# One load for the Q weights, the safe program laid ahead of each engine's last part, and the last output tile opened earlier, in a one-core attention kernel

## The chip, the core and the metric

The kernel runs on one core of a Trainium2 chip. The core has TensorE (PE in the profile, with PEld for its weight loads), VectorE (DVE), ScalarE (ACT), GpSimd (POOL) and SyncE (SP). They share an on-chip memory, and PE writes its results to eight accumulator banks (PSUM) of 128 x 512 float32. SP and ScalarE issue the transfers to and from the chip's main memory, which 16 DMA engines carry out. The instructions of each engine come from main memory as well, and the profile lists the packets that fetch them as queues of the kind "instruction". The metric is the device time of one execution in microseconds, as the median of several runs.

## The reference

A multi-head attention block with one sequence of 2048 rows, 448 features and 16 heads of 28 features. Inputs are bfloat16: `x` [1, 2048, 448], `wqkv` [448, 1344], `wo` [448, 448].

```python
qkv = transpose((x @ wqkv).reshape(B, S, 3, H, Dh), (2, 0, 3, 1, 4))
q, k, v = qkv[0], qkv[1], qkv[2]
scores = einsum("bhqd,bhkd->bhqk", q, k) * (Dh ** -0.5)
p = softmax(scores, axis=-1)
o = einsum("bhqk,bhkd->bhqd", p, v)
out = transpose(o, (0, 2, 1, 3)).reshape(B, S, D) @ wo
```

## The kernel before

The launch holds two programs. `_fast` computes the softmax without subtracting a maximum; at its end it checks that all row sums lie in a safe interval and writes the answer to `FLAG`. `_general`, the safe program, computes the same with a maximum and is run only where the check fails. `body` (line 1608) lays both out for each engine: the engine's instructions of `_fast`, a wait for `FLAG`, a load of its value into a register (line 1611), a branch (line 1612) to the label `done_` of that engine or to its `safe_` block, then the safe program, then `done_`. With the given inputs the branch to `done_` is taken. The safe program is long, and it lies between the branch and its target. A branch can be given a hint: `emit_engine` marks a place in an engine's stream ahead of the operation named in `HINT_AT`, and the hint instruction stands there (line 292; for GpSimd at the end of its operations, line 315). Behind `done_`, SP waits for the output's transfers (line 1627), and all engines meet in a final barrier (L1594 in the profile, a drain and semaphores).

**The order of work** is made by a planner written in Python, `_Prog.schedule`, which runs when the kernel is built. Each operation has an engine, its dependencies, an estimated duration and a priority (a lower number goes first). On each engine the planner takes, among the operations that can start within 150 ns of the first, the one with the lowest priority number, and among equals the one that was added first. PE's accumulator banks come from pools. Where the plan leaves PE a gap, it fills in passes on zeros (`zero_pass`, line 463), which serve only to keep PE's clock up. The order so found is fixed: each engine runs its list in order, waiting on semaphores.

**Loads** (lines 423 to 437). `x` comes in pieces of 256 or 512 rows, `wqkv` in three parts t = 0 (Q), 1 (K), 2 (V), seen as four row blocks of 112. In the order of issue SP loads x rows 256 to 511, the second halves of K's and Q's weights, x 512 to 1023, x 1024 to 1535, V's weights, x 1536 to 2047, then 16 pieces of `wo`. ScalarE issues x rows 0 to 255 and the first halves of K's and Q's weights.

**Head.** PE transposes x (`tr_job`, line 527: one job is one row block of 112 features for 512 rows), VectorE or ScalarE copies the result out of PSUM to `xT`, PE multiplies it with the weights (`proj_qk`, line 544: four steps of four matmuls that run side by side; `proj_v`, line 561), and the results are copied to `QT`, `KT`, `V`. For the first 512 rows the transposed block 1 is copied by ScalarE, the other three by VectorE; K's and Q's first projections have the same priority, Q's is added first and copied by ScalarE, K's by VectorE. These jobs take their banks from a pool of three. Later projections are spread over the rest of the run.

**Main part.** The work has 16 units: four groups of four heads, times four chunks of 512 query rows. A unit has 64 score tiles of 128 keys x 512 queries (16 key tiles, 4 heads). PE makes the scores (line 854), and ScalarE exponentiates three tiles at a time (two in unit 0), line 877; the operations are named E0, E1, and so on. About one tile in eight goes to VectorE instead, which evaluates a polynomial (lines 899 to 919). PE then multiplies the exponentials with V and adds over the 16 key tiles in one bank: the passes PV{unit}_{key tile}, line 810. A column of ones in V gives the row sums.

**Behind each unit** (`post_unit`): VectorE copies the sums out, SP sends them through main memory (`L1_`, `L2_`, `L3_`, `L4_`), VectorE takes reciprocals and normalizes (`NM{unit}`, line 733). When the last head group of a query chunk is done, PE multiplies with `wo` (line 703), VectorE copies the output tile out (`OPEV{tile}`, line 691) and SP stores it (`ODMA{tile}`, line 693).

**Tail** (`last_unit`). The last unit, 15, ends with output tiles 12 to 15. PE opens each of them with the product over the first three head groups (`OPA{tile}_{group}`, line 752, priority -34.0), as banks are free. The row sums go through PE here (N1 and N2, lines 771 and 786), VectorE normalizes in two halves (`NM15_0`, `NM15_1`), PE adds the last group (`OPB12` to `OPB15`, line 795, priority -35), ScalarE copies and stores tiles 12 and 14, VectorE copies tiles 13 and 15 and SP stores them. The check is a matmul on PE (`CKS`, line 947, priority -34.5) and one instruction on VectorE that writes `FLAG` (line 950). PE's order at the end is OPA12, OPA13, PV15_15, OPA14, N1, N2, OPB12, OPB13, OPB14, CKS, OPA15, OPB15.

Of the kernel before, what the change touches and what calls it, by code (L numbers as in the profile page):

```python
# [62 lines left out]
class _Prog:  # L63
# [12 lines left out]
    WINDOW = 3413.0  # L76
    FILL = None
    HINT_AT = {}
    FILL_DUR = 235.0
    FILL_ACT = 512.0  # L80
    FILL_TARGET = 5600.0
# [202 lines left out]
                    c += 1  # L284
                    op.count = c

    def emit_engine(self, e, engine, sems):
        waited = {}
        hint = None
        for op in self.order[e]:  # L290
            if op.name == self.HINT_AT.get(e):
                hint = engine.mark_branch_hint_location()
            need = {}
            for d in op.deps:
                if d.dma_group is not None:
                    key = ("dma", id(d.dma_group))
                    val = 16 * d.dma_index
                    sem = d.dma_group.sem
                else:
                    key = ("eng", d.eng)  # L300
                    val = d.count
                    sem = sems[d.eng]
                if waited.get(key, 0) >= val:
                    continue
                if key not in need or need[key][1] < val:
                    need[key] = (sem, val)
            for key, (sem, val) in need.items():
                engine.wait_ge(sem, val)
                waited[key] = val
            ins = op.emit(engine)  # L310
            if op.dma_group is not None:
                ins.then_inc(op.dma_group.sem, 16)
            elif op.sig:
                ins.then_inc(sems[e], 1)
        return engine.mark_branch_hint_location() if hint is None and self.HINT_AT else hint


RLO = 2.0 ** -40
# [18 lines left out]
def _fast(nc, x, wqkv, wo, out, n_heads=16):  # L337
# [28 lines left out]
    NU = len(units)  # L366
# [3 lines left out]
    P = _Prog()  # L370
    es = ExitStack()
    with es:
# [53 lines left out]
        def load_w(en, t, i0, i1):  # L426
            return load(en, (lambda e: e.dma_start(w_raw[0:IT, i0:i1, t * D:(t + 1) * D], wview[:, i0:i1, t * D:(t + 1) * D])),  # L427
                        f"w{t}_{i0}", (i1 - i0) * IT * D * 2)
        dma_x.append([load_x("act", 0, 2), load_x("sp", 2, 4)])
        for t in (1, 0):  # L430
            dma_w[t] = [load_w("act", t, 0, 2), load_w("sp", t, 2, 4)]
        dma_x.append([load_x("sp", 4, 8)])
        dma_x.append([load_x("sp", 8, 12)])
        dma_w[2] = [load_w("sp", 2, 0, 4)]
# [134 lines left out]

        for c in range(NCH):  # L570
            for it in range(NIT):
                tr_job(4 * c, it, -3 + 0.001 * it if c == 0 else 0.25 * c - CFG["klead"] + 0.001 * it, "act" if (c == 0 and it == 1) else "dve")
            if c == 0:
                proj_qk(0, 0, 0, -2.9, True, "act")
                proj_qk(1, 0, 0, -2.9, True, "dve")
            else:
                proj_qk(1, 0, c, 0.25 * c - CFG["klead"] + 0.05, True)
            proj_v(0, c, 0.25 * c + CFG["vlag"], True)
# [162 lines left out]
        def last_unit(u, last_pv):  # L741
            g, c = units[u]
            ub = u % 2
            pr = u - 50.0
            open_ops = []
            for j in range(NQT):
                n = c * NQT + j
                hold = []

                for gg in range(G - 1):  # L750
                    def f_part(e, n=n, hold=hold, gg=gg):
                        return e.matmul(bank(hold[0].banks[0])[:, 0:D], OTN[:, gg, n * 128:(n + 1) * 128], wop[:, gg, :],  # L752
                                        start=(gg == 0), stop=False, skip_group_check=True)
                    op = P.add("pe", f_part, deps=([otn_ev[(g_, c)] for g_ in range(G - 1)] + dma_wo[-1:] + mid_ev) if gg == 0 else [], after=hold[-1:], kind="f", units=0.9, act=448.0,
                               prio=-34.0, name=f"OPA{n}_{gg}", acq=("T", 1) if gg == 0 else None)
                    if gg == 0:
                        hold.append(op)
                open_ops.append((n, hold, op))
            HF = QCH // 2
            evs = []  # L760
            for k in range(2):
                sl = slice(k * HF, (k + 1) * HF)
                evs.append(P.add("dve", (lambda e, sl=sl: e.tensor_copy(OTS[:, ub, sl], bank(pv_open[u].banks[0])[:, sl])),
                                 deps=[last_pv, ots_last[ub]], after=evs[-1:], dur=340, prio=pr, name=f"ACCEV{u}_{k}", rel=[(pv_open[u], 0)] if k else []))
            n1s, rss, n2s, nms = [], [], [], []
            for k in range(2):
                def f_n1(e, k=k):
                    b = n1s[k].banks[0]
                    ins = None
                    for qt in (2 * k, 2 * k + 1):  # L770
                        ins = e.matmul(bank(b)[:, qt * 4:(qt + 1) * 4], OTS[:, ub, qt * 128:(qt + 1) * 128], SEL[:, :], start=True, stop=True)  # L771
                    return ins
                n1s.append(P.add("pe", f_n1, deps=[evs[k], sel_op], after=n1s[-1:], dur=430, prio=pr, name=f"N1_{u}_{k}", acq=("T", 1)))
            for k in range(2):
                i0 = u * 16 + 8 * k
                rss.append(P.add("dve", (lambda e, k=k, i0=i0: e.reciprocal(RS[:, i0:i0 + 8], bank(n1s[k].banks[0])[:, 8 * k:8 * k + 8])),
                                 deps=[n1s[k]], after=rss[-1:], dur=120, prio=pr, name=f"RS{u}_{k}", rel=[(n1s[k], 0)]))
                rs_last.append(rss[-1])

                def f_n2(e, k=k):  # L780
                    b = n2s[k].banks[0]
                    ins = None
                    for qt in (2 * k, 2 * k + 1):
                        for h in range(4):
                            i = u * 16 + qt * 4 + h
                            ins = e.matmul(ps[32 * h:32 * h + 32, b * 512 + qt * 128:b * 512 + (qt + 1) * 128],  # L786
                                           RS[:, i:i + 1].to_broadcast([128, 32]), id_f[:, :], start=True, stop=True, tile_position=(0, 32 * h))
                    return ins
                n2s.append(P.add("pe", f_n2, deps=[rss[k]], after=n2s[-1:], dur=480, prio=pr, name=f"N2_{u}_{k}", acq=("M", 1)))
                sl = slice(k * HF, (k + 1) * HF)  # L790
                nms.append(P.add("dve", (lambda e, sl=sl, k=k: e.tensor_tensor(OTN[:, g, c * QCH + sl.start:c * QCH + sl.stop], bank(n2s[k].banks[0])[:, sl], OTS[:, ub, sl], ALU.mult)),  # L791
                                 deps=[n2s[k]], after=nms[-1:], dur=340, prio=pr, name=f"NM{u}_{k}", rel=[(n2s[k], 0)]))
            for j, (n, hold, op) in enumerate(open_ops):
                def f_fin(e, n=n, hold=hold):
                    return e.matmul(bank(hold[0].banks[0])[:, 0:D], OTN[:, g, n * 128:(n + 1) * 128], wop[:, g, :], start=False, stop=True, skip_group_check=True)  # L795
                fin = P.add("pe", f_fin, deps=[nms[j // 2]], after=[op], kind="f", units=0.9, act=448.0, prio=pr, name=f"OPB{n}")
                out_tile(n, fin, hold[0], "act" if j % 2 == 0 else "dve", pr)

        def pv(u, kt):
# [154 lines left out]
        P.FILL = zero_pass  # L954
        P.START, P.COLD, P.HOT_UNTIL = 750.0, 7500.0, 10500.0
        n0 = (NCH - 1) * NQT
        P.HINT_AT = {"pe": f"OPA{n0}_0", "dve": f"OPEV{n0 - 1}", "act": f"OPEV{n0}", "sp": f"ODMA{n0 + 1}"}
        P.schedule()

        P.assign()  # L960
# [629 lines left out]
def _mha(nc, x, wqkv, wo, out, n_heads=16):  # L1590
# [3 lines left out]
    with es:  # L1594
# [11 lines left out]
        block = es.enter_context(nc.Block())  # L1606

        def body(e, eng):
            hint = F.emit_engine(e, eng, fs)
            eng.wait_ge(fs["dve"], F.flag_op.count)  # L1610
            ok = eng.value_load(F.flag_ap)
            eng.br_ne(ok, 0, on_true=f"done_{e}", on_false=f"safe_{e}").branch_hint(hint)
            with nc.body(f"safe_{e}", valid_engines=[eng.engine]):
                if e == "sp":
                    for gr in F.finish:
                        eng.wait_ge(gr.sem, 16 * gr.n)
                eng.drain().then_inc(bar, 1)
                eng.wait_ge(bar, 5)
                R.emit_engine(e, eng, rs)
                if e == "sp":  # L1620
                    for gr in R.finish:
                        eng.wait_ge(gr.sem, 16 * gr.n)
                eng.br(f"done_{e}")
            nc.switch_bb(f"done_{e}")
            if e == "sp":
                for gr in F.finish:
                    eng.wait_ge(gr.sem, 16 * gr.n)
# [52 lines left out]
```

## Time and profile before

| what | value |
|---|---|
| median of 3 runs | 421.03 us (420.53 to 422.55) |
| the profiled execution's own time | 424.5 us |
| its span, first to last instruction | 422.7 us |
| granted clock of PE, mean over the span | 0.996 |
| busy: PE, VectorE, ScalarE, GpSimd | 380.2, 385.5, 402.9, 3.4 us |
| ScalarE's exponentials | 307, 399.4 us in all |
| instruction packets, queue q8 and queue q14 | 36 and 13 |

The profiled execution is one run; its span leaves out 1.8 us of its own time, and it is 3.5 us above the median of the other runs. In a row of the profile "L877 ACT ACTIVATE PT<-ps" means: line 877 of the kernel, on ScalarE, reads `ps` (PSUM) and writes `PT`. "[2.51 <-PE ps L854]" means that the engine had been idle for 2.51 us and that an instruction of line 854 on PE ended it. An engine with a small q, as in SPq, is the engine's sequencer, which issues transfers, waits and branches.

### The profile page before, as it was taken

Reading aid. Unit: us, or ns where it says so; the run is one execution under the profiler, and the core shown is the slowest. Engines: PE = TensorE matmul, PEld = TensorE weight load, DVE = VectorE, ACT = ScalarE, POOL = GpSimd, SP = SyncE. Lnnn points to the kernel's source line nnn. Section 1 sums busy time; section 2 is a strip of 40 time slices with the busy share of each in tenths; the row PEclk is TensorE's granted clock in tenths of the full one; section 3 lists DMA queues with packets and bytes.
Section 4 is the critical chain, followed back from the end, with each engine's and each line's share of the span. In section 5 each row is a group of like instructions: output and inputs, shape, how many; then the busy total and the mean of one; then the engine's idle time right before and its main releaser. Section 6 shows DMA issues by size and latency. Waiting matters only on the chain.

```text
span 422.7 us, 9986 instructions
## 1 busy us (share of the span) xinstructions
PE 380.2 (90%) x4419; PEld 122.4 (29%) x4419; DVE 385.5 (91%) x608; ACT 402.9 (95%) x312; POOL 3.4 (1%) x9
## 2 busy tenths in 40 slices
PE   6999898899999898998989899989989998898895
PEld 3433222322323223232322222223222322222232
DVE  4489999999999999999999999999999999999923
ACT  2799999999999999999999999999999999999991
POOL 3000000000000000000000000000000000000000
PEclk9899999999999999999999999999999999999999
DMA  8200000101010000100001010000000001100111
GB/s 262 65 2 2 5 26 3 27 0 29 2 26 5 4 26 2 29 2 18 13 3 27 2 28 2 4 26 4 27 2 27 2 6 25 36 28 24 59 44 51
DMA packets 13897, 10.28 MB, mean 24 GB/s; under 512 B 5980, under 2 KB 11868, under 8 KB 13848
## 3 DMA queue, kind: packets, MB, share of 16 engines
q1 hardware_dynamic: 12808, 8.72, 7.6%
q10 hardware_dynamic: 1040, 0.86, 0.6%
q8 instruction: 36, 0.59, 0.6%
q14 instruction: 13, 0.11, 0.1%
HBM read 7.50 MB, written 2.08 MB: 23 GB/s over the span
## 4 chain that ended last, share of the span: by engine, by line
ACT 93%; PE 3%; DMA 2%; DVE 0%; ACTq 0%; issue 0%
ACT PT L877 93%; DMA w_raw<-in_wqkv_dram 2%; PE ps L544 1%; PE ps L752 1%; PE ps L854 0%; PE ps L810 0%; PE ps L527 0%; PE ps L795 0%; PE ps L703 0%; PE ps L771 0%; PE ps L463 0%; DVE OUTS L691 0%; PE ps L786 0%; ACTq L427 0%; ACTq L424 0%; DVE OTN L791 0%
## 5 line engine op out<-in xcount | busy, mean ns | idle before, releaser
L877 ACT ACTIVATE PT<-ps 128x1536 bf16<-128x1536 f32 (+1 forms) x307 | 399.4, 1797 | 2.5 <-PE ps L854 2.5
L854 PE MATMUL ps<-QT,KT 28*128 28x512 bf16 x1024 | 152.5, 384 | 31.4 <-ACT PT L877 28.2
L463 PE MATMUL ps<-ZM,ZW 128*32 128x512 bf16 x1404 | 113.8, 388 | 1.4 <-DVE ZM L445 1.2
L810 PE MATMUL ps<-PT,V 128*32 128x512 bf16 x890 | 96.0, 388 | 2.3 <-DVE OTS L716 1.1
L899 DVE TENSOR_SCALAR DT<-ps 128x512 f32<-128x512 f32 x134 | 91.3, 684 | 2.7 <-PE ps L854 1.5
L854 PEld LDWEIGHTS ps<-QT,KT 28*128 28x128 bf16 x1024 | 37.4, 91 | 164.9 <-ACT PT L877 130.8
L919 DVE SCALAR_TENSOR_TENSOR PD<-DT,DU 128x1024 int16<-128x1024 f32 x67 | 81.7, 1219 | 1.2
L810 PE MATMUL ps<-PD,V 128*32 128x512 bf16 x134 | 50.9, 388 | 0.0
L917 DVE TENSOR_TENSOR DU<-DU,DW 128x1024 f16<-128x1024 f16 x67 | 46.2, 689 | 1.7
L913 DVE TENSOR_TENSOR DU<-DW 128x1024 f16<-128x1024 f16 x67 | 46.0, 686 | 1.5
L911 DVE TENSOR_SCALAR DW<-DT 128x1024 f16<-128x1024 uint16 x67 | 45.5, 680 | 0.2
L463 PEld LDWEIGHTS ps<-ZM,ZW 128*32 128x32 bf16 x1404 | 34.7, 96 | 37.3 <-issue 19.9
L810 PEld LDWEIGHTS ps<-PT,V 128*32 128x32 bf16 x890 | 23.9, 93 | 51.5 <-issue 39.0
L544 PE MATMUL ps<-xT,w_raw 112*32 112x512 bf16 x512 | 35.3, 390 | 2.0 <-DMA w_raw<-in_wqkv_dram 1.8
L915 DVE TENSOR_SCALAR DU<-DU 128x1024 f16<-128x1024 f16 x67 | 27.9, 416 | 0.8
L515 DVE CAST KT<-ps 128x512 bf16<-128x512 f32 x16 | 11.0, 685 | 7.6 <-PE ps L544 7.4
L561 PE MATMUL ps<-w_raw,xT 112*128 112x112 bf16 x256 | 16.4, 214 | 0.2 <-DVE DT L899 0.2
L544 PEld LDWEIGHTS ps<-xT,w_raw 112*32 112x32 bf16 x512 | 11.5, 97 | 16.4 <-issue 3.5
L691 DVE CAST OUTS<-ps 128x448 bf16<-128x448 f32 x14 | 8.7, 622 | 7.2 <-PE ps L703 6.6
L561 PEld LDWEIGHTS ps<-w_raw,xT 112*128 112x128 bf16 x256 | 12.9, 98 | 5.9 <-issue 4.2
L810 PEld LDWEIGHTS ps<-PD,V 128*32 128x32 bf16 x134 | 12.1, 93 | 7.8 <-issue 6.6
L703 PE MATMUL ps<-wop,OTN 128*128 128x448 bf16 x48 | 11.3, 355 | 0.0
(47 smaller groups left out, 96.0 us busy)
## 6 DMA issues: line engine op xcount, KB each, us to landing
RB<-scr_r SPq DMA_DIRECT2D x60, 64.0 KB, 2.0
out_dram<-OUTS SPq DMA_DIRECT2D x14, 112.0 KB, 1.7
x_nat<-in_x_dram SPq DMA_DIRECT2D x3, 448.0 KB, 8.9
w_raw<-in_wqkv_dram SPq DMA_DIRECT2D x2, 196.0 KB, 5.3
w_raw<-in_wqkv_dram ACTq DMA_DIRECT2D x2, 196.0 KB, 5.7
w_raw<-in_wqkv_dram SPq DMA_DIRECT2D x1, 392.0 KB, 9.6
wop<-in_wo_dram SPq DMA_DIRECT2D x16, 24.5 KB
scr_l<-OTS SPq DMA_DIRECT2D x15, 8.0 KB
```

Source lines behind the costliest of these rows:

```text
L463: ins = e.matmul(ps[32 * h:32 * h + 32, b * 512:(b + 1) * 512], ZW[:, :], ZM[:, :], start=shut, stop=shut, skip_group_check=not shut, tile ...
L544: ins = e.matmul(ps[32 * h:32 * h + 32, b * 512:(b + 1) * 512], w_raw[0:IT, it, col:col + 32], xT[0:IT, it, c * 512:(c + 1) * 512], start= ...
L561: ins = e.matmul(ps[:, b * 512 + j * GD:b * 512 + (j + 1) * GD], xT[0:IT, it, n * 128:(n + 1) * 128], w_raw[0:IT, it, 2 * D + g * GD:2 * D ...
L810: ins = e.matmul(ps[32 * h:32 * h + 32, b * 512:(b + 1) * 512], V[:, kt, hh * 32:(hh + 1) * 32], p_ap, start=(kt == 0), stop=(kt == NK - 1 ...
L854: ins = e.matmul(bank(b), KT[32 * h:32 * h + rows, g, kt * 128:(kt + 1) * 128], QT[32 * h:32 * h + rows, g, c * QCH:(c + 1) * QCH], start= ...
L877: ex = P.add("act", (lambda e, p0=p0, w=w, bf=bf: e.activation(PT[:, p0 * 512:(p0 + w) * 512], bank(bf(), w), AF.Exp, scale=ESCALE)), deps ...
L899: o1 = P.add("dve", (lambda e, T1=T1, s=s: e.tensor_scalar(T1, bank(s.banks[0]), ZLO, ZOFF, ALU.max, ALU.add)), deps=[s, d_last[di]], dur= ...
L911: o2 = P.add("dve", (lambda e, F16=F16, W=W: e.tensor_scalar(W, F16, ES, EC, ALU.mult, ALU.add)), deps=[o for _, o, _ in pair] + [d_last[d ...
L913: o3 = P.add("dve", (lambda e, W=W, U=U: e.tensor_tensor(U, W, W, ALU.mult)), deps=[o2], dur=65 + n * 0.521, prio=pr, name=f"D3_{gi}")
L915: o4 = P.add("dve", (lambda e, U=U: e.tensor_scalar(U, U, EP, None, ALU.add)), deps=[o3], dur=65 + n * 0.261, prio=pr, name=f"D4_{gi}")
L917: o5 = P.add("dve", (lambda e, W=W, U=U: e.tensor_tensor(U, U, W, ALU.mult)), deps=[o4], dur=65 + n * 0.521, prio=pr, name=f"D5_{gi}")
L919: o6 = P.add("dve", (lambda e, U=U, T=T, O=O: e.scalar_tensor_tensor(O, T, ZFIN, U, ALU.add, ALU.add)), deps=[o5] + [slot_last.get(("D", q ...
```

## The change

Three things are changed.

- **Loads.** The Q weights come in one load of all four row blocks, issued by SP behind its half of K's weights and ahead of x's rows from 512 on; ScalarE's load of them is gone. The copy of the transposed block 1 moves from ScalarE to VectorE. K's first projection goes ahead of Q's (priorities -2.9 and -2.8).
- **Layout.** Each engine's stream is cut ahead of one operation (`JUMP_AT`; for GpSimd behind its last). There an unconditional branch goes to a new label `tail_`, and the safe program stands between this branch and the tail. The rest of the fast program follows at `tail_`, and behind it the wait for `FLAG`, the load of its value, the branch, and directly behind the branch the label `done_`. The cut is ahead of PV8_11 on PE, OPEV11 on VectorE, E0 on ScalarE, and the first `L1_0` on SP. A hint for the new branch is given on PE (ahead of PV8_8) and on VectorE (ahead of NM14); the others have none, and the closing branch has none.
- **Tail.** OPA's priority becomes -34.9, and that of OPB14 and OPB15 becomes -34.8.

```diff
-        for t in (1, 0):
-            dma_w[t] = [load_w("act", t, 0, 2), load_w("sp", t, 2, 4)]
+        dma_w[1] = [load_w("act", 1, 0, 2), load_w("sp", 1, 2, 4)]
+        dma_w[0] = [load_w("sp", 0, 0, 4)]
...
-                tr_job(4 * c, it, -3 + 0.001 * it if c == 0 else 0.25 * c - CFG["klead"] + 0.001 * it, "act" if (c == 0 and it == 1) else "dve")
+                tr_job(4 * c, it, -3 + 0.001 * it if c == 0 else 0.25 * c - CFG["klead"] + 0.001 * it, "dve")
             if c == 0:
-                proj_qk(0, 0, 0, -2.9, True, "act")
                 proj_qk(1, 0, 0, -2.9, True, "dve")
+                proj_qk(0, 0, 0, -2.8, True, "act")
...
-                               prio=-34.0, name=f"OPA{n}_{gg}", acq=("T", 1) if gg == 0 else None)
+                               prio=-34.9, name=f"OPA{n}_{gg}", acq=("T", 1) if gg == 0 else None)
...
-                fin = P.add("pe", f_fin, deps=[nms[j // 2]], after=[op], kind="f", units=0.9, act=448.0, prio=pr, name=f"OPB{n}")
+                fin = P.add("pe", f_fin, deps=[nms[j // 2]], after=[op], kind="f", units=0.9, act=448.0, prio=pr if j < 2 else -34.8, name=f"OPB{n}")
...
-        P.HINT_AT = {"pe": f"OPA{n0}_0", "dve": f"OPEV{n0 - 1}", "act": f"OPEV{n0}", "sp": f"ODMA{n0 + 1}"}
+        P.HINT_AT = {"pe": "PV8_8", "dve": f"NM{NU - 2}"}
+        P.JUMP_AT = {"pe": "PV8_11", "dve": f"OPEV{n0 - 1}", "act": "E0", "sp": "L1_0"}
...
+            def jump(hint):
+                br = eng.br(f"tail_{e}")
+                if hint is not None:
+                    br.branch_hint(hint)
+                with nc.body(f"safe_{e}", parent=top, valid_engines=[eng.engine]):
...
+                nc.switch_bb(f"tail_{e}", parent=top)
+
+            F.emit_engine(e, eng, fs, jump)
             eng.wait_ge(fs["dve"], F.flag_op.count)
             ok = eng.value_load(F.flag_ap)
-            eng.br_ne(ok, 0, on_true=f"done_{e}", on_false=f"safe_{e}").branch_hint(hint)
...
-            nc.switch_bb(f"done_{e}")
+            eng.br_ne(ok, 0, on_true=f"done_{e}", on_false=f"safe_{e}")
+            nc.switch_bb(f"done_{e}", parent=top)
```

In `emit_engine` the call `jump(hint)` comes ahead of the operation named in `JUMP_AT`, or behind the engine's last one where none is named.

More of the change, by code (lines that the diff above doesn't have):

```diff
@@ L78 @@
     HINT_AT = {}
+    JUMP_AT = {}
     FILL_DUR = 235.0
@@ L285, in assign, with emit_engine @@
                     op.count = c
-    def emit_engine(self, e, engine, sems):
+    def emit_engine(self, e, engine, sems, jump=None):
         waited = {}
@@ L292, in emit_engine @@
                 hint = engine.mark_branch_hint_location()
+            if op.name == self.JUMP_AT.get(e):
+                jump(hint)
+                jump = None
             need = {}
@@ L314, in emit_engine @@
                 ins.then_inc(sems[e], 1)
-        return engine.mark_branch_hint_location() if hint is None and self.HINT_AT else hint
+        if jump is not None:
+            jump(hint)
 RLO = 2.0 ** -40
@@ L1608, in body @@
         def body(e, eng):
-            hint = F.emit_engine(e, eng, fs)
+            top = nc.cur_bb
+            def jump(hint):
[3 more added lines that the diff above has]
+                with nc.body(f"safe_{e}", parent=top, valid_engines=[eng.engine]):
+                    if e == "sp":
+                        for gr in F.finish:
+                            eng.wait_ge(gr.sem, 16 * gr.n)
+                    eng.drain().then_inc(bar, 1)
+                    eng.wait_ge(bar, 5)
+                    R.emit_engine(e, eng, rs)
+                    if e == "sp":
+                        for gr in R.finish:
+                            eng.wait_ge(gr.sem, 16 * gr.n)
+                    eng.br(f"done_{e}")
+                nc.switch_bb(f"tail_{e}", parent=top)
+            F.emit_engine(e, eng, fs, jump)
             eng.wait_ge(fs["dve"], F.flag_op.count)
             ok = eng.value_load(F.flag_ap)
[L1612 to L1623, printed above, removed]
-            nc.switch_bb(f"done_{e}")
+            eng.br_ne(ok, 0, on_true=f"done_{e}", on_false=f"safe_{e}")
+            nc.switch_bb(f"done_{e}", parent=top)
             if e == "sp":
```

## The prediction

> **What bounds the kernel now.** I read the page first (the chain that ended last, the costliest groups, the queues), then the first 16 us and the last 20 us in order of time, then the branches and the transfers around them.
>
> ```profile
> span 422.7 us, 9986 instructions
> ...
> q8 instruction: 36, 0.59, 0.6%
> ...
> ACT 93%; PE 3%; DMA 2%; DVE 0%; ACTq 0%; issue 0%
> ...
> L877 ACT ACTIVATE PT<-ps 128x1536 bf16<-128x1536 f32 (+1 forms) x307 | 399.4, 1797 | 2.5 <-PE ps L854 2.5
> ```
>
> ScalarE's exponentials are 93% of the chain, and 2.5 us before the first of them is all the idle time ahead of 307. Nothing in the change makes an exponential shorter or fewer. What can move is when the first one starts, what comes after the last, and whether a jump in the middle breaks the row. In order of time, the head (start, duration, engine, line):
>
> ```profile
> 2.24 1.03 SPq L424 DMA_DIRECT2D x_nat<-in_x_dram  x2
> 8.85 2.67 PE L544 MATMUL ps<-xT,w_raw 112*32 112x512 bf16 x28 [1.82 <-DMA w_raw<-in_wqkv_dram]
> 10.44 0.17 PEld L544 LDWEIGHTS ps<-xT,w_raw 112*32 112x32 bf16 x4 [0.26 <-issue]
> 11.45 1.10 PE L527 MATMUL ps<-id_b,x_nat 128*112 128x128 bf16 x8
> 12.96 0.39 PE L854 MATMUL ps<-QT,KT 28*128 28x512 bf16 x4
> 13.39 17.52 ACT L877 ACTIVATE PT<-ps 128x1024 bf16<-128x1024 f32 x19 [2.51 <-PE ps L854]
> ```
>
> The first exponential starts at 13.39. Behind it stand the Q weights (PE waits until 8.85), 28 projection matmuls, transposes of the next x rows (11.45), one pass on zeros and the first scores at 12.96. The tail, first in order of time, then the closing branch (L1612), the first instruction behind it (L1594), and SP's wait for the last store:
>
> ```profile
> 410.36 0.62 DVE L691 CAST OUTS<-ps 128x448 bf16<-128x448 f32 x1 [2.30 <-PE ps L703]
> 415.96 0.80 PE L795 MATMUL ps<-wop,OTN 128*128 128x448 bf16 x3
> 416.79 0.74 PE L752 MATMUL ps<-wop,OTN 128*128 128x448 bf16 x3
> 417.37 0.35 PE L795 MATMUL ps<-wop,OTN 128*128 128x448 bf16 x1
> 417.76 0.62 DVE L691 CAST OUTS<-ps 128x448 bf16<-128x448 f32 x1 [0.53 <-PE ps L795]
> L1612 PEldq COMPARE_BRANCH  x1: 396/396/396, 417.8 to 417.8; - x1
> L1612 DVEq COMPARE_BRANCH  x1: 84/84/84, 418.5 to 418.5; - x1
> L1612 ACTq COMPARE_BRANCH  x1: 68/68/68, 419.2 to 419.2; - x1
> L1594 PEldq DRAIN  x1: 62/62/62, 418.3 to 418.3; - x1
> L1594 ACTq DRAIN  x1: 81/81/81, 420.2 to 420.2; - x1
> L1594 DVEq DRAIN  x1: 58/58/58, 422.2 to 422.2; - x1
> SPq L1627 <- DMA out_dram<-OUTS: 2.4, 1, 2.4
> ```
>
> All arithmetic is over at 417.76 + 0.62 = 418.4, and the span ends at 422.7: 4.3 us go to the closing branch and the last stores. Two things end together at 422.2. VectorE branches at 418.5 and runs the instruction behind the branch only at 422.2, 3.7 us later; ScalarE needs 1.0 (419.2 to 420.2), PE 0.5. And SP waits 2.4 us for the last output. How long the output stores take to land, and the instruction packets of the same stretch. The store issued at 408 us:
>
> ```profile
> out_dram<-OUTS SPq DMA_DIRECT2D x1, 112.0 KB, 1.7
> ```
>
> That of 411 us, with one instruction packet in the stretch to 412.9:
>
> ```profile
> q8 instruction: 1, 0.02, 4.1%
> ...
> out_dram<-OUTS SPq DMA_DIRECT2D x1, 112.0 KB, 3.5
> ```
>
> That of 417.2, ahead of the branches, and then the last, issued at 418.4, with the packets from 418.35 to the end:
>
> ```profile
> out_dram<-OUTS SPq DMA_DIRECT2D x1, 112.0 KB, 2.0
> ```
>
> ```profile
> q14 instruction: 6, 0.05, 3.1%
> q8 instruction: 1, 0.02, 2.2%
> ...
> out_dram<-OUTS SPq DMA_DIRECT2D x1, 112.0 KB, 3.8
> ```
>
> With no instruction packet beside it a store lands after 1.7 us; with a single one it took 3.5, and the last, among seven, 3.8. So the closing branches seem to cost twice: the fetch itself, and the late share of the last store that runs beside the fetches.
>
> **The change, part by part.** *The tail.* With the safe program moved ahead, the final branch goes to the instruction behind it, so neither the 3.7 us of VectorE nor the fetches should be there. PE's order also changes: OPA15 (priority -34.9) comes ahead of OPB14 and OPB15 (-34.8) and of the check CKS (-34.5). OPB12 and OPB13 stay at 415.96 and 0.2 later; OPA15's three matmuls take 416.79 to 417.37 = 0.58 now and would run from 416.36; OPB14 follows at 416.94, OPB15 at 417.14, 0.23 before 417.37. Tile 14's product is later than now, but done near 417.3, before VectorE's last copy. That copy and SP's last store, now at 417.76 + 0.62 + 0.03 = 418.41, move by 0.23: the store starts at 418.18. FLAG now falls behind that copy, near 418.3; every engine's closing branch waits for it, but SP reads it only after issuing its store, and the other engines have until the store lands. I let it land after 2.0, the row of the same stage: 420.2 instead of 422.2. Term: **-2.0 us**; bounds with 1.7 (419.9, -2.3) and 3.5 (a fetch still beside it: 421.7, -0.5).
>
> *The loads.* ScalarE loses one of its w_raw issues, SP's Q load doubles; the bytes ahead of x's next rows are the same. The times to landing of SP's half and ScalarE's half of Q now, and of x's next rows (issued at 2.24), and the two stretches that follow (busy times by engine, then granted clock, DMA share, GB/s):
>
> ```profile
> w_raw<-in_wqkv_dram SPq DMA_DIRECT2D x1, 196.0 KB, 6.6
> x_nat<-in_x_dram SPq DMA_DIRECT2D x1, 448.0 KB, 8.1
> w_raw<-in_wqkv_dram ACTq DMA_DIRECT2D x1, 196.0 KB, 7.0
> ```
>
> ```profile
> 6.01:9.42 3.41, 1.39 (x23) 0.74 (x25) 0.76 (x2) 0.47 (x1) 0.00 (x0) 1.00 1.07 350
> 9.42:12.83 3.41, 3.41 (x36) 1.52 (x24) 1.26 (x3) 0.60 (x1) 0.00 (x0) 0.50 0.88 229
> ```
>
> ScalarE's half ends PE's wait at 8.85; SP's, 0.4 faster, is there near 8.4, x at 10.35. In one queue the second half follows the first directly instead of sharing the engines with x: 8.5, nearer to the first row. A lower bound is 1.1 earlier (392 KB at 350 GB/s with no queue of x beside it), an upper 8.85. K's 16 matmuls now go first and hide in the wait of 1.82 us. The copy that moves from ScalarE to VectorE lies in VectorE's wait for PE: nothing. Q's four groups start at 8.5; a group takes 0.17 + 0.26 = 0.43 at half clock (the row at 10.44) and half of that at full, so three steps and one matmul of 0.39 end at 9.55, and Q's copy can start at 9.6, well before the 11.5 at which the 28 matmuls end now. Before the first scores PE still has the transposes, which wait for x at 10.35; from their start to the end of the scores it is 12.96 + 0.39 - 11.45 = 1.9 at half clock, about half at full. PE could feed ScalarE at 11.3 to 12.3.
>
> *ScalarE's jump.* It stands between Q's copy and the first exponential, with no hint. The sequencer reaches it when the copy's wait is over, 9.6. No jump without a hint is in the trace; the rows give 0.5 (PE), 1.0 (ScalarE) and 3.7 (VectorE), all hinted; the third looks like a fetch from scratch. I take 3.7, since nothing can have fetched the target: 13.3 instead of 13.39. Term: **-0.1 us**; bounds -2.1 (a jump of at most 1.0, PE at 11.3) and +1.0 (Q at 8.85, half clock, 3 x 0.43 + 0.6 = 1.9, jump from 10.7 to 14.4). So the gain of the loads is spent on the jump. [...]
>
> *PE's jump* at PV8_11 in the ninth unit of sixteen, near 13.4 + 399.4 x 0.55 = 232 us, has a hint three passes earlier, some 4.7 us. At the end PE's hinted branch cost 0.5. In 220 to 240 us PE waits for ScalarE anyway (total, times, longest):
>
> ```profile
> PEld ps L854 <- ACT PT L877: 5.6, 11, 0.7
> ```
>
> 0.5 a time, so 0.5 hides: **0**; bounds 0 and rival four. *VectorE's jump* before OPEV11: VectorE waits there for 2.30 us now, after a copy of 0.6 that was under way when the sequencer got free, 2.9 in all. A hit costs nothing; a miss of 3.7 makes that copy 0.8 late, which holds the bank of the last scores and so PE's chain to the end: up to +0.8. I take **0**, for its hint is a unit's normalization earlier. SP jumps before its first L1, which waits for the first unit to end, POOL when its memsets are over: 0.
>
> Sum: -2.0 - 0.1 = -2.1. The profiled execution's span of 422.7 becomes 420.6, and its own 424.5 becomes 422.4; it ran 3.5 above the median of 421.03, so the forecast for the median is 421.03 - 2.1 = **418.9 us**. Half a per cent, what can be told from no change, is 2.1 us: the forecast sits on that bound.
>
> **Rivals.** *One: ScalarE's jump is cheap*, 0.5 to 1.0 as in PE's and ScalarE's rows. Then the first exponential follows PE at 11.3 to 12.3, and the total is -3.1 to -4.1: 416.9 to 417.9. Against it: no hint. *Two: the loads come late or the clock is half*, as it was granted from 9.42 on after a stretch with PE busy 1.39 of 3.41: first exponential at 14.4, -2.0 + 1.0: 420.0. *Three: the layout does not free the tail.* The q8 packets are 36 in 422.7 us, one in 11.7, so one falls into the last 2.5 us about one time in five, and the last store again takes 3.5: -0.5 - 0.1, 420.4. *Four, slower: PE's jump misses.* VectorE's hinted jump took 3.7 all the same. A PE stall of 3.7, less the 0.9 that an exponential (399.4 / 307 = 1.3) leaves after its scores (0.4), idles ScalarE for 2.8; the idle stretch then brings half clock for 3.41 us, which hold 2.6 exponentials, 1.3 of PE's waits and 2.1 of its work; at half clock 1.7 of that is done, so about 0.4 more is lost: 3.2 - 2.1 = +1.1, 422.1, and more if the block behind the target has to be fetched as well (another 1.0 to 3.7). It decides once the stall is over 2 us.
>
> **How the numbers follow.** Forecast 0.42 (own range 418.1 to 419.7), rival one 0.18, two 0.14, three 0.13, four 0.13. Faster by over 0.5%: all of one and six in ten of the forecast, 0.43; slower by over 0.5% (over 423.1): four with a second fetch and the far end of two, 0.11; the rest 0.46. The range leaves out the far half of one and the far half of four: 417.2 to 422.6.
>
> **What would show it.** Right: no instruction packets beside the last store, which lands in 1.7 to 2.0; VectorE's last drain near 419; OPA15 ahead of OPB14; ScalarE's first exponential near 13.3 with the scores done a microsecond before. Wrong: scores and exponential back to back near 12 (one) or after 13.5 (two); a q8 packet after 417 us and a landing of 3.5 (three); ScalarE idle near 232 us (four).

## The result, and the profile after

The changed kernel takes 450.52 us as the median of four runs (443.43 to 456.62), against 421.12 for the kernel before. The ratio of 1.0595 (95% interval 1.0467 to 1.0723) is taken without the two longest executions, whose time and lower granted clock put them in a slower state. The change is clearly slower; 418.9 was forecast and the range ended at 422.6. The profiled execution is the fastest of the four, 443.43 with a span of 441.6, so the traces explain 22.3 of the 29.4 us (443.43 less 421.12); the rest lies between executions of this one kernel.

The page of the kernel after (all line numbers are higher by five or six from here on: L859 for L854, L882 for L877): the span, the clock in 40 slices, and the exponentials with the idle time ahead of them.

```profile
span 441.6 us, 9986 instructions
...
PEclk9555569999999999999999999998999999999999
...
L882 ACT ACTIVATE PT<-ps 128x1536 bf16<-128x1536 f32 (+1 forms) x307 | 403.3, 1672 | 21.0 <-PE ps L859 15.6
```

The 307 exponentials take 403.3 us against 399.4, but ScalarE now idles 21.0 us ahead of them instead of 2.5, most of it (15.6) waiting for scores, and the clock stands at half for slices 2 to 5. The head in order of time:

```profile
7.48 0.55 PEld L549 LDWEIGHTS ps<-xT,w_raw 112*32 112x32 bf16 x16 [0.34 <-DMA w_raw<-in_wqkv_dram]
...
8.58 0.60 ACT L516 ACTIVATE QT<-ps 128x512 bf16<-128x512 f32 x1 [5.50 <-PE ps L549]
...
9.39 0.40 PE L859 MATMUL ps<-QT,KT 28*128 28x512 bf16 x4
...
14.23 2.85 ACT L882 ACTIVATE PT<-ps 128x1024 bf16<-128x1024 f32 x3 [5.06 <-issue]
15.31 0.10 PEld L859 LDWEIGHTS ps<-QT,KT 28*128 28x128 bf16 x2 [4.89 <-ACT PT L882]
15.31 0.60 PE L859 MATMUL ps<-QT,KT 28*128 28x512 bf16 x2 [4.40 <-ACT PT L882]
```

The Q weights are there at 7.5 and the first scores at 9.8, earlier than I had them. ScalarE takes its jump when it starts Q's copy, and its next instruction runs only at 14.23: 5.6 us for the jump, 4.4 of them after the scores. And PE, whose banks are full, stands still for 4.40. What that does is in the stretches (length, busy time and instructions of PE, PEld, DVE, ACT, POOL, then granted clock, DMA share, GB/s), after:

```profile
12.75:63.95 51.20, 48.64 (x318) 15.55 (x322) 27.25 (x44) 35.98 (x34) 0.00 (x0) 0.50 0.02 4
63.95:299.47 235.52, 212.29 (x2589) 65.33 (x2581) 226.67 (x350) 235.31 (x176) 0.00 (x0) 1.00 0.05 14
299.47:302.88 3.41, 3.34 (x28) 0.72 (x28) 3.23 (x7) 1.57 (x2) 0.00 (x0) 0.50 0.00 0
```

and before:

```profile
12.83:64.00 51.17, 49.19 (x553) 17.27 (x549) 45.10 (x76) 50.61 (x48) 0.00 (x0) 1.00 0.05 11
```

From 9.34 to 12.75 PE is busy for only 1.57 of 3.41 us, and then the clock is granted at half for 51.2 us, fifteen times 3.41. PE is busy for 48.64 of them and gets through 318 matmul records instead of 553; ScalarE is busy for 36 us instead of 50.6, and what it waits for is PE's scores. PE is the bound there. The granted clock of this trace changes at 12.75, 63.95, 299.47 and 302.88, whole multiples of 3.413 us apart; a stretch of 3.41 us counted from these times is called a window below. In the first of the fifteen windows PE was busy for 0.85 us, in each of the other fourteen all through, and full clock came back only behind the last of them, at 63.95.

Compared exponential by exponential, the first starts 0.84 later than in the trace of before, the 37th 18.6 later, and the lag grows by 2.4 more near 300 us. The last starts 20.8 later, and from there to the end the kernel after needs 8.83 us instead of 10.66. The tail after (the new branch, the closing one, the first instructions behind it, SP's last wait, and the stores of the last stretch):

```profile
L1618 ACTq COMPARE_BRANCH  x1: 33/33/33, 8.6 to 8.6; - x1
L1618 PEldq COMPARE_BRANCH  x1: 330/330/330, 251.9 to 251.9; - x1
L1618 DVEq COMPARE_BRANCH  x1: 80/80/80, 428.2 to 428.2; - x1
...
L1637 DVEq COMPARE_BRANCH  x1: 70/70/70, 439.6 to 439.6; - x1
...
L1600 DVEq DRAIN  x1: 17/17/17, 439.7 to 439.7; - x1
...
L1641 SPq EVENT_SEMAPHORE  x2: 17/22/28, 440.5 to 440.8; - x2
...
out_dram<-OUTS SPq DMA_DIRECT2D x2, 112.0 KB, 1.8
```

VectorE runs on 0.1 us behind its closing branch, not 3.7; the stores land in 1.8 us, with no instruction packet beside them. That part does what the prediction said.

### The profile page after: what moved, and what is told of

Same layout as the page of the kernel before. It is cut to its first block, busy times and chain, and to the rows that moved or that the text cites. A ratio compares the mean times of both kernels' runs of the same rounds, so it can differ in the third digit from the quotient of the medians.

```text
span 441.6 us, 9986 instructions
## 1 busy us (share of the span) xinstructions
PE 397.8 (90%) x4419; PEld 124.9 (28%) x4419; DVE 386.8 (88%) x609; ACT 406.3 (92%) x311; POOL 3.4 (1%) x9
## 3 DMA queue, kind: packets, MB, share of 16 engines
q1 hardware_dynamic: 13032, 8.93, 7.3%
## 4 chain that ended last, share of the span: by engine, by line
ACT 58%; DVE 19%; PE 17%; DMA 3%; issue 1%; SPq 1%; DVEq 0%
ACT PT L882 58%; PE ps L859 5%; DVE DT L904 4%; DVE PD L924 4%; PE ps L815 3%; DVE DU L918 2%; PE ps L549 2%; DVE DU L922 2%; PE ps L468 2%; DVE DW L916 2%; DMA RB<-scr_r 2%; DMA scr_r<-RS 2%; PE ps L566 2%; PE ps L532 2%; DVE DU L920 1%
## 5 line engine op out<-in xcount | busy, mean ns | idle before, releaser
L882 ACT ACTIVATE PT<-ps 128x1536 bf16<-128x1536 f32 (+1 forms) x307 | 403.3, 1672 | 21.0 <-PE ps L859 15.6
L859 PE MATMUL ps<-QT,KT 28*128 28x512 bf16 x1024 | 160.1, 402 | 31.9 <-ACT PT L882 28.8
L468 PE MATMUL ps<-ZM,ZW 128*32 128x512 bf16 x1404 | 115.2, 392 | 1.2 <-DVE ZM L450 1.2
L815 PE MATMUL ps<-PT,V 128*32 128x512 bf16 x890 | 100.2, 407 | 6.4 <-DVE PD L924 3.3
L859 PEld LDWEIGHTS ps<-QT,KT 28*128 28x128 bf16 x1024 | 36.7, 91 | 169.4 <-ACT PT L882 117.8
L815 PE MATMUL ps<-PD,V 128*32 128x512 bf16 x134 | 52.4, 400 | 0.8 <-DVE PD L924 0.8
L468 PEld LDWEIGHTS ps<-ZM,ZW 128*32 128x32 bf16 x1404 | 34.8, 97 | 38.3 <-issue 21.7
L549 PE MATMUL ps<-xT,w_raw 112*32 112x512 bf16 x512 | 37.4, 407 | 0.2
L520 DVE CAST KT<-ps 128x512 bf16<-128x512 f32 x16 | 11.0, 685 | 11.4 <-PE ps L549 11.3
L566 PE MATMUL ps<-w_raw,xT 112*128 112x112 bf16 x256 | 19.3, 234 | 0.0
L566 PEld LDWEIGHTS ps<-w_raw,xT 112*128 112x128 bf16 x256 | 15.0, 108 | 8.2 <-issue 5.5
L520 DVE CAST V<-ps 128x448 bf16<-128x448 f32 x16 | 9.9, 618 | 6.0 <-PE ps L566 6.0
```

The lines of the kernel that those rows point to most:

```text
L468: ins = e.matmul(ps[32 * h:32 * h + 32, b * 512:(b + 1) * 512], ZW[:, :], ZM[:, :], start=shut, stop=shut, skip_group_check=not shut, tile ...
L549: ins = e.matmul(ps[32 * h:32 * h + 32, b * 512:(b + 1) * 512], w_raw[0:IT, it, col:col + 32], xT[0:IT, it, c * 512:(c + 1) * 512], start= ...
L566: ins = e.matmul(ps[:, b * 512 + j * GD:b * 512 + (j + 1) * GD], xT[0:IT, it, n * 128:(n + 1) * 128], w_raw[0:IT, it, 2 * D + g * GD:2 * D ...
L815: ins = e.matmul(ps[32 * h:32 * h + 32, b * 512:(b + 1) * 512], V[:, kt, hh * 32:(hh + 1) * 32], p_ap, start=(kt == 0), stop=(kt == NK - 1 ...
L859: ins = e.matmul(bank(b), KT[32 * h:32 * h + rows, g, kt * 128:(kt + 1) * 128], QT[32 * h:32 * h + rows, g, c * QCH:(c + 1) * QCH], start= ...
L882: ex = P.add("act", (lambda e, p0=p0, w=w, bf=bf: e.activation(PT[:, p0 * 512:(p0 + w) * 512], bank(bf(), w), AF.Exp, scale=ESCALE)), deps ...
```

## The experiments

The theory after these traces (T in the expectations): ScalarE's jump starves PE, the clock falls to half, and at half clock PE is the bound and does not get full clock back. Rivals: the new loads and order of the head (U); a lasting cost of the code behind a jump (V).

**ScalarE's jump ahead of Q's copy.** Edit of the changed kernel:

```diff
-P.JUMP_AT = {..., "act": "E0", "sp": "L1_0"}
+P.JUMP_AT = {..., "act": "p0_0_0_ev", "sp": "L1_0"}
```

> Only ScalarE's jump moves, from ahead of E0 to ahead of Q's copy, where ScalarE is idle anyway. Theory T (the jump ahead of E0 starves PE for 4.4 us, the granted clock falls to half, and PE at half clock is then too slow to earn it back): first exponential at 9.8 to 10.3, clock full from 10 us on, tail as in the changed kernel (1.8 us shorter than before), 415 to 417 us. Rival U (the new order of the head leaves PE too little work, jump or not): half clock from about 13 us on for tens of us, 430 or more. Rival V (running from a block that was jumped to costs ScalarE something lasting): 430 or more with a full clock.

Measured: 426.22 us, ratio 1.0108 (1.0037 to 1.0179). The first exponential, the stretch to 64 us, and later in the same trace VectorE's normalization and the exponentials around 280 us:

```profile
9.85 9.27 ACT L882 ACTIVATE PT<-ps 128x1024 bf16<-128x1024 f32 x10 [0.69 <-PE ps L859]
...
9.85:64.00 54.15, 51.67 (x583) 17.95 (x583) 48.48 (x79) 54.15 (x50) 0.00 (x0) 1.00 0.09 24
...
276.89 0.69 DVE L738 TENSOR_TENSOR OTN<-RB,OTS 128x512 bf16<-128x512 f32 x1 [1.67 <-DMA RB<-scr_r]
...
280.65 1.45 ACT L882 ACTIVATE PT<-ps 128x1536 bf16<-128x1536 f32 x1 [1.72 <-PE ps L859]
```

One edit brings back 24 us: the jump falls into ScalarE's idle time, the first exponential starts at 9.85, and the clock is full up to 279.6 us. The tail stays at 8.83. But the kernel is still about 1% slower than before, not the 415 to 417 us that were expected: against a second trace of the kernel before (below) it loses 7.2 us between 245 and 325 us at three places, about 0.8, 5.0 and 1.4. At the second, the transfers of 269.9 to 271.0, with SP's store of the reciprocals:

```profile
q8 instruction: 1, 0.02, 7.7%
...
scr_r<-RS SPq DMA_DIRECT2D x1, 8.0 KB, 3.5
```

A packet of queue q8, taken for PE's code, starts at 270.97, and the 8 KB of reciprocals beside it land after 3.5 us instead of the usual 1.4. The four broadcasts `RB` are issued only then, VectorE waits 1.67 for them, behind it PE 2.1 for VectorE's polynomial, ScalarE 1.72 for PE, and half clock follows from 279.6 to 289.8. In the changed kernel itself the 2.4 us near 300 are the same: packet at 291.96, `scr_r` landing after 3.0. At the first place a packet at 246.87 falls beside the broadcasts, one of which lands after 3.3 instead of 2.0. The third, 1.39 us ahead of the 239th exponential, follows a single window of half clock at 320.5 without a late transfer.

**PE kept busy during the stall.** The changed kernel with 22 passes on zeros (of four matmuls) on PE ahead of its third scores; they are extra work.

```diff
+            if op.name == "S2" and e == "pe" and self.PADDING:
+                self.PADDING(engine)
...
+            for _ in range(22):
+                for h in range(4):
+                    e.matmul(..., ZW[:, :], ZM[:, :], start=True, stop=True, tile_position=(0, 32 * h))
```

> The changed kernel with 22 passes on zeros (4.7 us) on PE ahead of S2, inside the time in which PE waits for the first exponential; ScalarE's jump stays where it is. T: first exponential still near 14.2, but full clock from there on; before's time + 0.8 at the head - 1.8 at the tail, 420 us, perhaps 1 to 2 more for a normalization that comes late. V: still 440 or more, since the jump is still there. U can't be told from T here.

Measured: 426.07 us, ratio 1.0108 (1.0073 to 1.0142). First exponential and the stretch that ran at half clock before:

```profile
14.34 3.84 ACT L885 ACTIVATE PT<-ps 128x1024 bf16<-128x1024 f32 x4 [4.93 <-issue]
...
12.75:63.95 51.20, 49.27 (x574) 17.54 (x566) 42.92 (x71) 49.61 (x47) 0.00 (x0) 1.00 0.05 11
```

The jump costs as much as in the changed kernel, yet the clock stays full, and 24 us are back. So it is PE's idling through the stall, not the stall, that costs most. The 420 us expected are missed by 6: the first exponential is 3.7 later than in the second trace of the kernel before (10.61), not 0.8, and 1.4 more are lost in the main part.

**The stall without a jump.** The kernel of the first experiment (jump early), with ten copies of 512 columns on ScalarE ahead of its first exponential, extra work.

```diff
+            if op.name == "E0" and e == "act" and self.STALL:
+                self.STALL(engine)
...
+            for i in range(10):
+                e.activation(STL[:, i * 512:(i + 1) * 512], ZM[:, :], AF.Identity)
```

> e1's kernel with ten copies of zeros (4.4 us) on ScalarE between the first scores and E0, so ScalarE is late by about as much as by the jump, but without a jump there; the copies go to a buffer that nothing reads. T: first exponential near 14.2, PE idle for 4 us, half clock for some 50 us, 435 to 455. V: no more than the stall itself, 420.

Measured: 453.32 and 444.58 us. First exponential and the stretch of half clock in the trace of the first (the other has a mean granted clock of 0.938, the same as the changed kernel's trace):

```profile
15.04 2.82 ACT L885 ACTIVATE PT<-ps 128x1024 bf16<-128x1024 f32 x3
...
15.70:73.80 58.10, 57.71 (x381) 17.07 (x381) 33.04 (x54) 41.08 (x38) 0.00 (x0) 0.50 0.02 3
```

PE stands for 5.2 us, and the loss is there; no jump is needed. In the first experiment ScalarE ran behind its jump all along and the loss was gone. Together that refutes a lasting cost of the code behind the jump.

**The loads alone, and the layout with the old loads.** The first puts the load edits (one Q load, the copy on VectorE, K first) into the kernel before, the second takes the same three out of the changed kernel.

```diff
-        for t in (1, 0):
-            dma_w[t] = [load_w("act", t, 0, 2), load_w("sp", t, 2, 4)]
+        dma_w[1] = [load_w("act", 1, 0, 2), load_w("sp", 1, 2, 4)]
+        dma_w[0] = [load_w("sp", 0, 0, 4)]
...
```

> The kernel before with the loads, the copy on VectorE and K's projection first, and nothing else of the change (no jump). T: Q's weights there near 7.5, first exponential near 9.8, full clock, tail as before: 421.1 - 3.5 = 417.6 us. U: half clock after the first exponential, 430 or more.

> The changed kernel with the loads, the copy and the order of K and Q as before: layout and tail alone. T: ScalarE's jump again stands between Q's copy (near 10 us) and E0; first exponential at 13.5 to 16, PE idle for 2 to 4 us, half clock after it for tens of us, 430 to 450 us. U (the loads and the order are the cause): clock full, near 421.

Measured: loads alone 422.79 us, ratio 1.003 (0.9984 to 1.0076); layout with the old loads 456.06 and 444.42 (mean granted clock 0.902 and 0.938). First exponential of the loads alone:

```profile
10.65 8.37 ACT L877 ACTIVATE PT<-ps 128x1024 bf16<-128x1024 f32 x9 [0.64 <-PE ps L854]
```

and the half clock of the layout with the old loads:

```profile
14.80:72.80 58.00, 57.73 (x381) 17.12 (x381) 33.00 (x54) 40.97 (x38) 0.00 (x0) 0.50 0.02 4
```

The loads neither lose nor gain what can be measured (417.6 was expected), and the layout, with the new order of the tail, has the whole loss.

**The kernel before once more**, without an edit, for a second trace of it.

> The kernel before once more, unchanged, for a second trace of it: the first was 3.5 us above its median. If that lay at the head and the tail, the first exponential is nearer to 11 and what follows the last one nearer to 9.5 us here (the span near 420); if it lay in the middle, they stay at 13.39 and 10.66.

Measured: 421.37 us, span 419.6, the last exponential's start 10.30 from the end. Its first exponential:

```profile
10.61 8.36 ACT L877 ACTIVATE PT<-ps 128x1024 bf16<-128x1024 f32 x9 [1.27 <-PE ps L854]
```

The execution whose rows I predicted from started 2.8 us later (13.39), with its Q weights late (8.85, here 7.64) and its clock at half; that delay and a tail 0.4 longer are what its span lies above this one by.

**PE's code blocks moved back.** In the trace of the kernel before a packet of queue q8 (16 KB) comes every 228 to 288 of PE's recorded instructions, 257 on average, up to the tail. Behind PE's jump the places where they fall, counted in instructions, differ between the kernels (in the kernel after 61 to 109 behind those of the kernel before, or about 170 ahead of the next), since the safe program stands ahead of the rest now. The kernel of the first experiment gets 86 instructions in PE's safe block, which are never executed and bring the blocks back to the places of the kernel before.

```diff
                     eng.wait_ge(bar, 5)
+                    for _ in range(86 if e == "pe" else 0):
+                        eng.drain()
                     R.emit_engine(e, eng, rs)
```

> e1's kernel with 86 drains added to PE's safe program, which never runs: they only move PE's tail against the 16 KB blocks of code, back to where the blocks of the kernel before began. Theory P (in e1 and in the changed kernel a code packet of PE ran beside a small transfer of a normalization, which landed 1.6 to 2 us later, held VectorE and then PE, and cost the clock): no wait over 1 us for RB or scr_r near 270 us, no half clock there, e1's time less the 7.2 us that it loses between the 165th and the 240th exponential, 417 to 419 us. Rival W (e1 loses that because ScalarE is 3.5 us ahead of VectorE, or by the jump itself): as e1, 424 to 429.

> The kernel with ScalarE's jump early and 86 padding instructions once more. Eight of its ten executions lay at 419.0 to 419.2; the profiled one had 422.8 and three single windows of half clock. If these windows belong to single executions and not to the kernel, the profile now has a span of 417.2 to 417.5, first exponential near 9.9, no gap over 1.7 us, and a tail of 8.8.

Measured: 419.09 us, ratio 0.9916 (0.988 to 0.9953), and in the second set 419.74, ratio 0.9936 (0.9876 to 0.9995). It beats both kernels, the kernel before by less than 1%. In the trace of the second set (span 417.2, clock full throughout), the row of exponentials through the second place above, and the transfers of 268.5 to 271.5:

```profile
260.04 24.98 ACT L882 ACTIVATE PT<-ps 128x1536 bf16<-128x1536 f32 x18
...
scr_r<-RS SPq DMA_DIRECT2D x1, 8.0 KB, 1.4
```

No packet falls there (the two around it start at 265.9 and 277.4), `scr_r` lands in 1.4, and ScalarE runs through. Between the medians, instructions that nobody executes are worth 6.5 to 7.1 us. Against the second trace of the kernel before, the first exponential is 0.9 earlier and the tail 1.5 shorter (8.83): 2.3 of span. The first set's trace (422.81, span 421.0) had single windows of half clock at 75, 191 and 317 us and lost 3.5 us there; why an execution gets them is open. The last of them again cost 1.3 us ahead of the 239th exponential, and so did one in the trace of the old tail order (below): the third place of the first experiment is such a window, which executions have with the padding too.

**Another place for the code blocks**: 214 instead of 86, half a block further.

> The kernel with ScalarE's jump early and 214 instead of 86 never-executed instructions in PE's safe block: PE's 256-instruction code blocks behind its jump lie 128 instructions off those of the kernel before. Theory of the code phase (it matters which instruction the code packet falls beside): packets land at other instructions than in both kernels, so the gaps at 251, 277 and 321 of the kernel with no padding are not at those places; the time is anywhere from 419 to 427, with gaps, where there are any, at packets beside a normalization transfer. Rival (any padding helps, or the jump into another page costs the same everywhere): 419 as with 86, or 426 as with 0, with the gaps at the same exponentials as in those.

Measured: 421.42 us (419.84 to 428.74), ratio 0.9964 (0.9907 to 1.0021). In its trace the transfers of 317 to 322.5, a packet at 319.72 among them, and what VectorE then waited for:

```profile
q8 instruction: 1, 0.02, 1.5%
...
scr_r<-RS SPq DMA_DIRECT2D x1, 8.0 KB, 3.2
...
DVE OTN L738 <- DMA RB<-scr_r: 1.3, 1, 1.3
```

The collision is at another unit, 50 us later than without padding, and costs ScalarE 0.7 in this execution: between these kernels the place of the packets decided. A late `scr_r` alone was no loss: in the second trace of the kernel before a packet at 218.94 lies beside one that lands after 2.4, and ScalarE runs on.

**No hint for PE's jump**, otherwise the kernel with the blocks moved back (87 padding instructions, since the hint is one less).

```diff
-        P.HINT_AT = {"pe": "PV8_8", "dve": f"NM{NU - 2}"}
+        P.HINT_AT = {"dve": f"NM{NU - 2}"}
```

> e7's kernel without the hint for PE's jump (87 drains, so that the blocks stay where they are). PE's jump then misses: PE stands for 2.5 to 4 us near 228 us; ScalarE is late by 2 to 3 us at once, and where the clock falls to half after it, by several more: 421 to 430 us. If the hint does nothing, as e7.

Measured: 426.3 us in a single run. PE's branch, and ScalarE behind it:

```profile
L1618 PEldq COMPARE_BRANCH  x1: 3676/3676/3676, 230.2 to 230.2; - x1
...
239.79 6.87 ACT L882 ACTIVATE PT<-ps 128x1536 bf16<-128x1536 f32 x5 [7.00 <-PE ps L859]
```

3.7 us in the branch, and then PE stands for another 3.3 in which it waits for nothing that the profile shows, taken here for the block behind the target: ScalarE idles 7.0. With the hint, in the changed kernel, a packet of q8 starts 1.2 behind the hint, the branch took 0.33 and ScalarE lost nothing, so PE's hint is served.

**A hint for ScalarE's jump**, the changed kernel otherwise:

```diff
+        P.HINT_AT = {..., "act": "p0_0_0_ev"}
```

> The change with one thing more: ScalarE's jump ahead of the first exponential gets a hint, given ahead of Q's copy, which ScalarE's sequencer reaches some 5 us before the jump. If the missing hint is what cost (theory one, the stall of ScalarE starves PE and the clock stays at half for 50 us): the first exponential at 9.8 to 10.1, full clock afterwards, span near 424.5 and 426 us in all, as with the jump moved ahead of the copy. If a hint is missed here as VectorE's was near 428 us (packet 8 us behind the hint all the same): first exponential near 14, span near 441, 444 to 456 us.

Measured: 450.01 us, ratio 1.0612 (1.0506 to 1.0719). The hint, the branch and the first exponential:

```profile
L293 ACTq BRANCH_PREFETCH_HINT  x1: 50/50/50, 1.8 to 1.8; - x1
...
L1618 ACTq COMPARE_BRANCH  x1: 52/52/52, 8.2 to 8.2; - x1
...
13.93 2.85 ACT L882 ACTIVATE PT<-ps 128x1024 bf16<-128x1024 f32 x3 [5.15 <-issue]
```

The hint runs 6.4 us ahead of the branch, and the jump costs 5.7 all the same. A hint at this place did not help; moving the jump did.

**The old order of the tail** in the kernel with the blocks moved back:

```diff
-                               prio=-34.9, name=f"OPA{n}_{gg}", ...)
+                               prio=-34.0, name=f"OPA{n}_{gg}", ...)
-                ... prio=pr if j < 2 else -34.8, name=f"OPB{n}")
+                ... prio=pr, name=f"OPB{n}")
```

> The kernel with ScalarE's jump early and 86 padding instructions, but with the priorities of the last output tiles as before (OPA -34.0, OPB14 and OPB15 like OPB12). If the tail's gain of 1.5 to 2.1 us is the layout's alone, the stretch from the last exponential's start to the end stays at 8.8; by the prediction's sum the order is worth 0.23, so 9.05 to 9.1.

Measured: 419.47 us, last exponential's start to the end 8.93 against 8.83. In these single traces the order is worth 0.1, the layout the rest.

## Why the prediction was wrong

- *The tail* (-2.0, bounds -2.3 and -0.5): right. 10.66 became 8.83, -1.8; against the second trace of before -1.5. The layout gives it, as argued (8.93 with the old order); of the 0.23 taken for the order 0.1 was found.
- *The loads* (Q at 8.5, PE ready at 11.3 to 12.3): no gain is shown. The one trace of before had a late head; in the second Q came at 7.64, and with the loads alone at 8.32, with first exponentials at 10.61 and 10.65. In the changed kernel Q came at 7.5 and the scores were ready at 9.8, earlier than forecast.
- *ScalarE's jump* (3.7, first exponential at 13.3): a miss, as argued, but of 5.6, taken from 8.6 to 14.23. The price of VectorE's row was carried to a place where the DMA engines were 83% busy with loads: the packet started 3.4 us behind the branch there, 1.05 behind VectorE's branch in the tail. That the loads held it up is argued from these two, not tested. The term, -0.1, came out as +0.84 against the same trace and as +3.6 against the second.
- *The step that failed* is the one behind the first exponential: the sum counts ScalarE's stall up to there and carries nothing of it further. Where the prediction prices half clock, in rivals two and four, it takes a few groups of Q or one window of 3.41 us, as in the row 9.42:12.83 of before. In the runs half clock lasted 51.2 us and cost 17.8, as the first three experiments show, and no case in the prediction contained it. The sum never asked what PE does while its banks are full: by its own times (PE ready at 11.3 to 12.3, first exponential at 13.3) PE would have stood for 1 to 2 us and then until that exponential freed a bank; it stood for 4.40. Why half clock then holds on for 51.2 us stays open.
- *PE's jump* (0): right for the jump (0.33, no loss). But the layout in front of PE's code moved every later packet, a term that was not in the sum: 2.4 us here, and 6.5 to 7.1 us between the medians of the kernels with 0 and with 86 padding instructions.
- *VectorE's jump* (0, bound +0.8): its hint, 7.3 us ahead, was missed again: the packet came at 429.27, behind the branch. The next copy started at 431.28, 3.0 behind the branch, but it waited for PE too: VectorE idled 2.44 ahead of it against 2.30 before, so the miss was hidden.
- SP's and POOL's jumps: 0, as said.

Worked out for the profiled executions, against the second trace of before (span 419.56 to 441.64, +22.1): first exponential +3.6, half clock after it +17.8, the event near 300 us +2.4, tail -1.5, and -0.2 of small differences. That the other three executions are 6 to 13 us slower still was not traced; the traces of the third experiment and of the old loads, at 453 and 456 us, have 58 us of half clock and further stretches of up to 13.7 us later.

## What to carry to other kernels

Ask of every stall what PE does meanwhile: price the clock that it loses (here half clock cost 17.8 us, the late first exponential 3.6), not only the wait, above all where PE has the projections to catch up with and little slack. Put a jump into idle time of its engine (here ahead of Q's copy instead of behind it, worth 24 us), or give PE something to run (22 passes on zeros were worth 24 us too). The change of layout moved the places of PE's code packets by about 170 instructions; where a small transfer is on a chain of waits, look at which packets fall beside it, and try to shift them with instructions that are never executed (86 of them were worth 6.5 to 7.1 us).

## What the runs showed of the hardware that was not expected

- Half clock outlasted its cause: PE stood for 4.40 us in the changed kernel, 5.17 in the stall without a jump and 3.75 in the layout with the old loads, and the half clock after it lasted 51.2, 58.1 and 58.0 us with PE 95 to 99% busy, so in these runs a high share of busy time alone did not bring full clock back. Nor did the number of matmul records in a window tell when it would come back. In the stall without a jump half clock went on behind a window with 30, and in the layout with the old loads full clock came back behind one with 31; but it also did behind one with 27 in the changed kernel (60.54) and one with 24 in the kernel without PE's hint (237.45). The two rows, first the window behind which it stayed at half:

```profile
46.46:49.88 3.42, 3.42 (x30) 1.17 (x28) 2.31 (x4) 2.36 (x3) 0.00 (x0) 0.50 0.00 0
...
195.72:199.13 3.41, 3.41 (x31) 0.85 (x32) 2.85 (x6) 3.15 (x3) 0.00 (x0) 0.50 0.03 5
```

  What brings full clock back stays open; no run tested it.
- One packet of PE's code (queue q8, 16 KB) beside an 8 KB transfer took that from 1.4 to 3.0, 3.2 and 3.5 us in three kernels where ScalarE then lost time, and to 2.4 in the kernel before (218.94), where it lost none.
- The jump over the safe program cost 5.6 to 5.7 us on ScalarE during the loads, at most 3.0 on VectorE in the tail, and 3.7 on PE without a hint, with 3.3 more of standing behind it. On PE, where the hint was given 5.4 us ahead, a packet of q8 came 1.2 behind the hint and the branch took 0.33; on ScalarE (6.4 ahead) the jump still cost 5.7, and on VectorE (7.3 ahead) the packet came 1.05 behind the branch.
